# Folding squares on GpSimd, quarter pieces, paired QK bursts and a plan ranked from behind, in a fused attention and highway-FFN kernel

## The chip, the cores and the metric

The kernel runs on one core of a Trainium2 chip. Times are device microseconds (us) of one launch. A profiled execution also gives the span from the first to the last instruction and the duration of each instruction on the engines: TensorE (PE, with its weight loads as PEld), VectorE (DVE), ScalarE (ACT), GpSimd (POOL) and SyncE (SP, which here only issues DMAs).

## The reference

```
q_n = q / (norm(q, axis=-1) + 1e-06);  k_n likewise      # q, k, v: 8 x 12 x 448 x 64
scores = q_n @ k_n^T / tau                               # tau = 0.1
attn = softmax(scores);  y = attn @ v
x = y.transpose(0, 2, 1, 3).reshape(3584, 768)
H = max(x @ w_h, 0);  T = sigmoid(x @ w_t + b_t)
out = T * H + (1 - T) * x
```

Eight batches of twelve heads go through cosine attention, and the 3,584 rows of 768 that come out go through a highway layer with two 768 x 768 weight matrices.

## The kernel before, in words

The attention works in **quads**: four heads of one batch, so 24 quads, three to a batch. For each quad, q and k (t = 0 and t = 1) are loaded in 14 groups of 64 numbers per partition each (`raw`). Their squares (`sq`, 14 x 64 per partition) are made by ACT for q and by POOL for k (DVE in quad 0), and DVE sums each square tile over 64 numbers in two instructions of 7 groups (L338). A reciprocal square root by an integer start value and Newton steps (`rs`, `ta`, L359 to L397) follows, for one quad at a time in the first two batches and for a whole batch later. POOL then multiplies q and k by it in one instruction of 896 numbers per partition each (`qn`, L420). The normalized tiles are turned by PE and copied out of PSUM (quads 0 to 3, `tp`, L440 to L449) or turned by a DMA (L458).

A quad's scores come in seven **chunks**. A chunk is four small matmuls into one of two score buffers in PSUM (`sp`, L505) and one exponential by ACT (`e`, L516). When all seven are there, 84 and then 28 matmuls multiply with v (`u`, L536, one PSUM buffer), and DVE divides by the sums (`rd`, `x`, `xtail`). v is cast to fp16 by DVE (`vm`, L474).

The FFN works in 28 **tiles** of 128 rows: three for each batch, and a fourth after every second batch for the rows left over. A tile is a transpose by PE (`xp`, 6 matmuls), a copy by DVE (`xT`, L642), four quarters of 6 or 7 matmuls of 384 columns (`pt`, L662; 26 per tile), a tanh by ACT (`tt`) or a maximum by DVE (`hm`, L687) behind each quarter, and two closing instructions by DVE per half (`th`, L703, and `o`, L711). The weights come in twelve loads (`wst`), each cast by DVE (`w`, L284), and every FFN matmul waits for all of them (`w_done`). A "batch" below, as a unit of work, is three quads and 3.5 tiles.

The order on each engine is not written by hand. Every operation is handed to a planner (`Plan`) with an engine, a planned duration, a due time (`pri`), and the operations it waits for. `run` simulates the engines greedily, taking at each step the operation that can start first and, among those that can start within 60 ns, the one due first. Its result is the fixed order on each engine. Due times are written out at each operation, mostly as an offset from `slot_t`, the planned start of a quad. The planner also lets POOL and those DVE instructions marked "lock" exclude each other.

Of the kernel before, what the change touches and what calls it, by code (L numbers as in the profile page):

```python
# [20 lines left out]
class Plan:  # L21

    LAT = {"PE": 260, "ACT": 170, "DVE": 150, "POOL": 150, "SP": 0}
    SWITCH = 93

# [22 lines left out]
    def run(self):  # L50
# [17 lines left out]
        ready = {e: [] for e in self.LAT}  # L68

# [18 lines left out]
        while len(order) < len(self.ops):  # L88
            best = None
            for e, L in ready.items():  # L90
# [4 lines left out]
                for r, o in L:  # L95
# [9 lines left out]
                    k = (max(s, t + 60), o.pri, o.n)  # L105
# [34 lines left out]
def kernel(  # L140
# [35 lines left out]
    rd_p = pool("rd", 3)  # L176
    qn_p = pool("qn", N_QN)
# [18 lines left out]
    NV = 2  # L196
    vm_b = [const.tile([128, 6, C, 66], FP16, name=f"vm{i}") for i in range(NV)]
# [37 lines left out]
    def load_qk(Q):  # L235
        b, qd = divmod(Q, NQ)
        ring, wait = P.buf("raw", N_RAW)
        pri = slot_t[Q] - 45
        st["ring_raw", Q] = ring
        got = []  # L240
        for t in range(2):
# [10 lines left out]
            o = op("SP", 60 if Q == 0 and t else 550, pri + 0.01 * t, wait, f, size=1300)  # L252
# [5 lines left out]
    def load_v(b):  # L258
# [10 lines left out]
        o = op("SP", 600, slot_t[NQ * b] - (34 if b else 14), wait, f, size=4000)  # L269
# [3 lines left out]
    w_done = []  # L273

    def load_w(i):
        ring, wait = P.buf("w", N_W)

        def f():
            st["wst", i] = wst_p.tile([128, DM], FP32, name="wst")
            src = (moe_w_h, moe_w_t)[i % 2]  # L280
            nc.sync.dma_start(st["wst", i][:, :], src[(i // 2) * 128 : (i // 2 + 1) * 128, :])

        def g():
            nc.vector.tensor_copy(w_f[i % 2][:, i // 2, :], st["wst", i][:, :])  # L284
# [4 lines left out]
        w_done.append(c)  # L289

    def load_b():
# [6 lines left out]
        a = op("SP", 430, 30, [], f, size=50)  # L298
        w_done.append(op("DVE", 470, 31, [a, o_fb], g))
# [505 lines left out]
```

## Time and profile before

| | us |
|---|---|
| median of 2 runs (346.66 to 347.35) | 347.0 |
| profiled execution: its own time | 349.8 |
| its span | 347.3 |
| PE busy / share of the span | 274.7 / 79% |
| DVE busy / share | 276.4 / 80% |
| ACT busy / share | 196.5 / 57% |
| POOL busy / share | 149.6 / 43% |

The shares are averages over stages that differ: FFN matmuls run only from 82.5 us on, POOL has nothing left to do from about 280 us on, and the last attention work ends near 318 us. The profiled execution is 2.8 us longer than the median of the runs, and 2.5 us of it lie outside the span.

### The profile page before, as it was taken

The numbers are of one execution on the slowest core, as the hardware profiler recorded it, in microseconds if no ns is written. First come the engines' busy times: TensorE is split into PE (matmuls) and PEld (weight loads), VectorE is DVE, ScalarE is ACT, GpSimd is POOL, SyncE is SP. The second block draws the span as 40 slices with busy tenths as digits, with TensorE's granted clock in tenths as the row PEclk, the third lists the DMA queues.
The fourth block names the chain that finished last, engine by engine and source line by source line (L and its number), as shares of the span: only waits on it lengthen the run. The fifth ranks groups of instructions, "written<-read, shape, count | busy, mean of one in ns | idle before, by whom it ended". The sixth has DMA issues, their size and how long they took to land.

```text
span 347.3 us, 10053 instructions
## 1 busy us (share of the span) xinstructions
PE 274.7 (79%) x4312; PEld 153.0 (44%) x4312; DVE 276.4 (80%) x505; ACT 196.5 (57%) x253; POOL 149.6 (43%) x147
## 2 busy tenths in 40 slices
PE   0076785569994889888976999799988999997982
PEld 0044452433551445443542555355454555454541
DVE  4999988956999899999998789776767665665663
ACT  3265865467382568656664586457765676770210
POOL 1438499289693803983386584333232000000000
PEclk9999756555996999999995999899989999998999
DMA  7999195999952767486798954154440641111112
GB/s 285 402 402 359 33 350 148 280 236 301 262 191 63 218 168 254 125 251 120 218 231 205 355 119 100 62 86 100 100 100 6 124 120 47 48 49 47 45 45 91
DMA packets 62318, 58.57 MB, mean 169 GB/s; under 512 B 38722, under 2 KB 57154, under 8 KB 62275
## 3 DMA queue, kind: packets, MB, share of 16 engines
q1 hardware_dynamic: 62002, 57.49, 57.6%
q8 instruction: 33, 0.54, 0.6%
q10 hardware_dynamic: 272, 0.46, 0.4%
q14 instruction: 11, 0.08, 0.1%
HBM read 37.75 MB, written 11.01 MB: 140 GB/s over the span
## 4 chain that ended last, share of the span: by engine, by line
PE 46%; DVE 46%; ACT 3%; issue 2%; DMA 1%; DVEq 0%
PE pt L662 28%; DVE n L338 9%; PE u L536 9%; DVE th L703 8%; PE sp L505 7%; DVE o L711 6%; DVE x L587 4%; DVE hm L687 4%; DVE vm L474 3%; ACT e L516 3%; DVE xT L642 2%; DVE rs L365 2%; PE xp L638 2%; DVE w L284 2%; DMA raw<-in_q_dram 1%
## 5 line engine op out<-in xcount | busy, mean ns | idle before, releaser
L516 ACT ACTIVATE e<-sp 128x896 f16<-128x896 f32 x168 | 149.0, 918 | 88.3 <-PE sp L505 87.9
L662 PE MATMUL pt<-w,xT 128*128 128x384 f16 x672 | 141.7, 342 | 16.8 <-DVE xT L642 14.4
L420 POOL TENSOR_TENSOR qn<-raw,rs 128x896 f16<-128x896 f32 x46 | 83.3, 1831 | 51.1 <-DMA qT<-qn 28.7
L662 PEld LDWEIGHTS <-xT 128*128 128x128 f16 x672 | 59.3, 101 | 70.6 <-issue 23.7
L505 PE MATMUL sp<-qT,qT 64*64 64x448 f16 x672 | 69.0, 426 | 15.7 <-ACT e L516 9.0
L536 PE MATMUL u<-vm,e 64*128 64x65 f16 x2688 | 60.6, 201 | 16.2 <-DVE x L587 14.0
L536 PEld LDWEIGHTS <-e 64*128 64x128 f16 x2688 | 52.3, 101 | 32.9 <-DVE x L587 15.2
L338 DVE TENSOR_REDUCE n<-sq 128x7 f32<-128x448 f16 x96 | 55.2, 605 | 9.4 <-ACT sq L326 7.6
L328 POOL TENSOR_TENSOR sq<-raw 128x896 f16<-128x896 f32 x23 | 40.4, 1761 | 43.4 <-DVE n L338 23.4
L703 DVE SCALAR_TENSOR_TENSOR th<-tt,hm 128x384 f16<-128x384 f16 x56 | 49.5, 890 | 2.7
L682 ACT ACTIVATE tt<-pt 128x384 f16<-128x384 f32 x56 | 27.5, 491 | 41.6 <-PE pt L662 41.5
L687 DVE SCALAR_TENSOR_TENSOR hm<-pt,x 128x384 f16<-128x384 f32 x48 | 26.6, 553 | 26.9 <-PE pt L662 26.4
L505 PEld LDWEIGHTS <-qT 64*64 64x64 f16 x672 | 19.7, 110 | 58.0 <-issue 47.6
L711 DVE SCALAR_TENSOR_TENSOR o<-x,th 128x384 f32<-128x384 f16 x48 | 36.0, 753 | 0.8
L326 ACT ACTIVATE sq<-raw 128x896 f16<-128x896 f32 x24 | 22.7, 951 | 5.8 <-DMA raw<-in_q_dram 5.8
L587 DVE TENSOR_TENSOR x<-u,rd 128x384 f16<-128x384 f32 x48 | 24.4, 549 | 0.5
L474 DVE CAST vm<-vr 128x896 f16<-128x896 f32 x24 | 22.6, 978 | 0.1
L440 PE MATMUL tp<-ident,qn 128*128 128x128 f16 x56 | 7.0, 297 | 17.8 <-DVE qn L420 17.7
L642 DVE COPY xT<-xp 128x768 f16<-128x768 f16 x28 | 15.4, 551 | 6.9 <-PE xp L638 6.6
L569 DVE RECIPROCAL rd<-u 128x12 f32<-128x12 f32 (+1 forms) x48 | 9.7, 202 | 13.4 <-PE u L536 13.1
L662 PE MATMUL pt<-bth,ones_row 128*128 128x384 f16 x56 | 19.1, 340 | 0.0
L391 POOL TENSOR_TENSOR ta<-rs,n 128x84 f32<-128x84 f32 (+1 forms) x18 | 8.0, 445 | 15.9 <-DVE rs L365 15.5
(35 smaller groups left out, 116.6 us busy)
## 6 DMA issues: line engine op xcount, KB each, us to landing
raw<-in_q_dram SPq DMA_DIRECT2D x24, 448.0 KB, 6.1
vr<-in_v_dram SPq DMA_DIRECT2D x8, 1344.0 KB, 7.4
raw<-in_k_dram SPq DMA_DIRECT2D x23, 448.0 KB, 6.0
out_dram<-o SPq DMA_DIRECT2D x24, 384.0 KB, 2.4
wst<-in_moe_w_h_dram SPq DMA_DIRECT2D x6, 384.0 KB, 4.5
wst<-in_moe_w_t_dram SPq DMA_DIRECT2D x6, 384.0 KB, 4.3
out_dram<-o SPq DMA_DIRECT2D x8, 192.0 KB, 2.7
qT<-qn SPq DMA_TRANSPOSE x40, 3.8
```

The source lines that it names most:

```text
L328: (nc.vector if eng == "DVE" else nc.gpsimd).tensor_mul(o, i, i)
L338: nc.vector.reduce_sum(n2[:, qd, g0 : g0 + C], st["sq", Q, t][:, C * part : C * part + C, :], axis=AX.X,)
L420: (nc.vector if eng == "DVE" else nc.gpsimd).tensor_mul(st["qn", Q, t][:, :, :].rearrange("p c (h d) -> p h c d", h=2), st["raw", Q][:, g, ...
L474: nc.vector.tensor_copy(vm[:, 2 * i : 2 * i + 2, :, 0:D], st["vr", b][:, 2 * i : 2 * i + 2, :].rearrange("p i (c d) -> p i c d", c=C),)
L505: nc.tensor.matmul(sp[64 * half : 64 * half + 64, h, 0:S].rearrange("x (c p) -> x c p", c=C), lhsT=kT[hp, ci, 64 * half : 64 * half + 64], ...
L516: nc.scalar.activation(e[:, o : o + 2 * S].rearrange("x (a p c) -> x a p c", a=2, c=C), st["sp", Q, ci][:, :, 0:S].rearrange("x a (c p) -> ...
L536: nc.tensor.matmul(u[:, s, slot * (D + 1) : (slot + 1) * (D + 1)], lhsT=e[sp, o : o + 128], rhs=vm[sp, 2 * qd + h, c, 0 : D + 1], start=(c ...
L587: nc.vector.tensor_mul(st["x", b][:, :, 4 * qd : 4 * qd + 4, :].rearrange("p t (h s) d -> p t h s d", s=2)[:, :, :, s, :], u[:, s, :, 0:D] ...
L662: nc.tensor.matmul(loc["pt", qi][:, :], lhsT=loc["xT"][:, cc, :] if cc < CC else ones_row[:, :], rhs=w_f[w_i][:, cc, ms] if cc < CC else b ...
L687: nc.vector.scalar_tensor_tensor(out=loc["hm"][:, ms], in0=loc["pt", qi][:, :], scalar=0.0, in1=xf()[:, ms], op0=ALU.max, op1=ALU.subtract,)
L703: nc.vector.scalar_tensor_tensor(out=loc["th", mh][:, :], in0=loc["tt"][:, ms], scalar=1.0, in1=loc["hm"][:, ms], op0=ALU.add, op1=ALU.mult,)
L711: nc.vector.scalar_tensor_tensor(out=loc["o"][:, ms], in0=xf()[:, ms], scalar=2.0, in1=loc["th", mh][:, :], op0=ALU.mult, op1=ALU.add,)
```

## The change

1. For quads 6 to 23 both squares are made by ACT. POOL then adds the upper 32 of each 64 squares to the lower 32 (two instructions of 7 groups, `sq` to `fold`, in fp32) and the upper 16 of these to the lower 16 (one instruction over 14 groups). DVE sums what is left, 14 groups of 16, in one instruction. Quads 0 to 5 keep the old sums.
2. POOL's other long instructions are cut: the squares that it still makes (quads 1 to 5) into two of 448, the normalizing products into four of 256 or 192.
3. The score matmuls of two consecutive chunks are issued together, when both score buffers are free.
4. The due time of most operations is no longer written down. It is worked out from behind: what an operation's consumers are due at, less 1.3 times its planned duration and hand-over. The planned spacing of quads is 7.5 us throughout. Loads and casts of the weights have fixed due times, those of `w_t` come first, and a quarter waits only for its own matrix.
5. A tile's transpose is created in the middle of the tile before it, and in quads 0 to 3 both turned tiles are copied by DVE (before, ACT copied one of the two).

```diff
@@ Plan
+    SLACK = 1.3
+    NEAR = {"PE": 100, "ACT": 100, "DVE": 60, "POOL": 60, "SP": 60}
...
+        while back:
+            o = back.pop()
+            due = 1e9 if o.pri is None else o.pri[0] if isinstance(o.pri, tuple) else o.pri
+            for c in outs[o.n] if not isinstance(o.pri, tuple) else ():
+                lat = o.dur + self.LAT[o.eng] + (o.size + 2000 if o.eng == "SP" else 0)
+                due = min(due, c.pri - (self.SLACK * lat / 1000 if o in c.deps else 0))
+            o.pri = due
...
-                    k = (max(s, t + 60), o.pri, o.n)
+                    k = (max(s, t + self.NEAR[e]), o.pri, o.n)
@@ kernel
+    FOLD = 6
+    PAIR = 0
...
-    slot_t = [T0 + (7.6 * Q if Q < NQ else 7.6 * NQ + 9.0 * (Q - NQ)) for Q in range(NQUAD + 2)]
+    slot_t = [14 + 7.5 * Q for Q in range(NQUAD + 2)]
@@ load_w
-            src = (moe_w_h, moe_w_t)[i % 2]
+            src = (moe_w_t, moe_w_h)[i // CC]
...
-        a = op("SP", 430, 13 + 1.4 * i, wait, f, size=1300)
-        c = op("DVE", 470, 14 + 1.4 * i, [a], g, kind="lock")
+        a = op("SP", 430, (12 + 1.8 * i,), wait, f, size=1300)
+        c = op("DVE", 470, (16 + 1.8 * i,), [a], g, kind="lock")
@@ squares
-            eng = "ACT" if t == 0 else ("DVE" if Q == 0 else "POOL")
+            eng = "ACT" if t == 0 or Q >= FOLD else "POOL" if Q else "DVE"
...
+                    nc.gpsimd.tensor_mul(o[:, 0:C, :], i[:, 0:C, :], i[:, 0:C, :])
+            def f2(t=t):
+                o, i = st["sq", Q, t][:, C:NT, :], st["raw", Q][:, NT * t + C : NT * t + NT, :]
+                nc.gpsimd.tensor_mul(o, i, i)
...
+            if Q < FOLD:
+                last = [(C * i, C, D, st_sq(Q, t), [both[i]]) for i in range(2)]
+            else:
+                last = [(0, NT, D // 4, st_fold(Q, t), folds(Q, t, a, ring))]
@@ folds (new)
+                nc.gpsimd.tensor_add(
+                    st["fold", Q, t][:, g, :], sq[:, g, 0 : D // 2], sq[:, g, D // 2 : D]
+                )
+            first.append(op("POOL", 460, None, [a] + ([("first", first)] if first else waitf), f))
+        def h():
+            x = st["fold", Q, t]
+            nc.gpsimd.tensor_add(
+                x[:, :, 0 : D // 4], x[:, :, 0 : D // 4], x[:, :, D // 4 : D // 2]
+            )
+        last = op("POOL", 460, None, first, h)
@@ norms
+            parts = [(0, 2, 0, C)] if eng == "DVE" else [
+                (h, h + 1, c0, c1) for h in range(2) for c0, c1 in ((0, 4), (4, C))
+            ]
...
-                    if t == 0:
-                        nc.scalar.copy(st["qT", Q, t][:, :, :], st["tp", Q, t][:, :, :])
-                    else:
-                        nc.vector.tensor_copy(st["qT", Q, t][:, :, :], st["tp", Q, t][:, :, :])
+                    nc.vector.tensor_copy(st["qT", Q, t][:, :, :], st["tp", Q, t][:, :, :])
@@ quad
+            pair.append((f, needs, ring_s, ring_qT))
+            if Q < PAIR or len(pair) == 2 or g_i == C * NQUAD - 1:
+                fs = [x[0] for x in pair]
...
+                a = op("PE", 400 if len(fs) == 2 else 205, None, sum((x[1] for x in pair), []), both,
+                       kind="quad")
@@ ffn
-                       [c] + ([("first", mms[:1])] if mms else waitq) + w_done, mm, kind="full")
+                       [c] + ([("first", mms[:1])] if mms else waitq) + w_done[w_i], mm, kind="full")
...
+            if qi == 2:
+                later()
```

What the planner makes of this is seen in the order of the instructions. The first place is DVE around the copy of the first FFN tile's transposed rows. Before:

```order
L579 TENSOR_TENSOR xtail<-u,rd 64x2x2x64
L642 COPY xT<-xp 128x768
L284 CAST w_109<-wst 128x768
L284 CAST w_110<-wst 128x768
L474 CAST vm_114<-vr 128x14x64 x3
L338 TENSOR_REDUCE n_672<-sq_968 128x7 x2
L569 RECIPROCAL rd<-u 128x12
```

and with the change:

```order
L669 TENSOR_TENSOR xtail<-u,rd 64x2x2x64
L730 COPY xT<-xp 128x768
L367 TENSOR_REDUCE n_1011<-fold_804 128x14
L367 TENSOR_REDUCE n_1011<-fold_981 128x14
L541 CAST vm_117<-vr 128x14x64 x2
L302 CAST w_112<-wst 128x768
L541 CAST vm_117<-vr 128x14x64
L782 SCALAR_TENSOR_TENSOR hm<-pt,x 128x384
L798 SCALAR_TENSOR_TENSOR th<-tt,hm 128x384
```

Both stand behind the third quad. Before, 4 of 12 weight casts stand ahead of the copy and the first `hm` comes 30 rows after it (two more quads lie between, on PE 18 chunks and 224 matmuls with v). Now 11 of 12 stand ahead of it, the first `hm` comes six rows after it, and one chunk pair lies on PE between the transpose and the end of the tile's first quarter.

The second place is POOL ahead of quad 6, the first of the third batch (`sq` squares, `ta` and `rs` the Newton steps for a batch, `qn` normalizing). Before:

```order
L328 TENSOR_TENSOR sq_1156<-raw 128x896
L393 TENSOR_TENSOR ta<-ta,rs 128x84
L395 TENSOR_SCALAR ta<-ta 128x84
L397 TENSOR_TENSOR rs<-ta,rs 128x84
L420 TENSOR_TENSOR qn_1186<-raw,rs 128x2x7x64
L420 TENSOR_TENSOR qn_1282<-raw,rs 128x2x7x64
L420 TENSOR_TENSOR qn_1291<-raw,rs 128x2x7x64
```

and with the change:

```order
L454 TENSOR_TENSOR ta<-ta,rs 128x84
L394 TENSOR_TENSOR fold_1398<-sq_1348 128x224
L456 TENSOR_SCALAR ta<-ta 128x84
L394 TENSOR_TENSOR fold_1398<-sq_1348 128x224
L458 TENSOR_TENSOR rs<-ta,rs 128x84
L394 TENSOR_TENSOR fold_1472<-sq_1364 128x224
L486 TENSOR_TENSOR qn_1503<-raw,rs 128x4x64 x2
L486 TENSOR_TENSOR qn_1511<-raw,rs 128x4x64 x2
L486 TENSOR_TENSOR qn_1503<-raw,rs 128x3x64 x2
L486 TENSOR_TENSOR qn_1511<-raw,rs 128x3x64 x2
```

The same stretch is now short instructions, and the squares are gone from it.

The third place is ACT near the middle of the program (`sq` squares, `e` exponentials, `tt` tanh). Before:

```order
L682 ACTIVATE tt<-pt 128x384
L326 ACTIVATE sq_3316<-raw 128x896
L516 ACTIVATE e_117<-sp 128x896 x2
L682 ACTIVATE tt<-pt 128x384
L516 ACTIVATE e_117<-sp 128x896 x3
L682 ACTIVATE tt<-pt 128x384
L516 ACTIVATE e_117<-sp 128x896
```

and with the change:

```order
L777 ACTIVATE tt<-pt 128x384
L343 ACTIVATE sq_3358<-raw 128x896
L586 ACTIVATE e_119<-sp 128x896 x2
L777 ACTIVATE tt<-pt 128x384
L343 ACTIVATE sq_3416<-raw 128x896
L586 ACTIVATE e_119<-sp 128x896
L586 ACTIVATE e_120<-sp 128x896
L343 ACTIVATE sq_3487<-raw 128x896
L586 ACTIVATE e_120<-sp 128x896 x2
```

Exponentials now come in twos, mostly with a square or a tanh between the twos.

## Rows read from the trace of the kernel before

**Rows 1.** The page's busy time: us, share of span, instructions.

```profile
PE 274.7 (79%) x4312; PEld 153.0 (44%) x4312; DVE 276.4 (80%) x505; ACT 196.5 (57%) x253; POOL 149.6 (43%) x147
```

**Rows 2.** Stages: start:end, length, busy PE, PEld, DVE, ACT, POOL, clock, DMA, GB/s.

```profile
57.00:82.50 25.50, 16.86 (x297) 9.03 (x294) 21.02 (x36) 16.63 (x21) 17.79 (x19) 0.50 0.90 259
82.50:220.00 137.50, 116.87 (x1826) 63.16 (x1823) 125.80 (x215) 83.44 (x110) 82.53 (x73) 0.92 0.72 192
220.00:341.50 121.50, 113.00 (x1708) 62.89 (x1704) 79.62 (x154) 65.16 (x88) 15.71 (x14) 0.96 0.28 70
```

**Rows 3.** DVE and PE around the first FFN tile: start, us, instruction.

```profile
56.96 0.56 DVE L642 COPY xT<-xp 128x768 f16<-128x768 f16 x1
...
82.47 2.10 PE L662 MATMUL pt<-w,xT 128*128 128x384 f16 x6
```

**Rows 4.** PE in the late stage, start, us, instruction: one batch.

```profile
270.94 0.38 PE L505 MATMUL sp<-qT,qT 64*64 64x448 f16 x4
271.26 1.51 PE L536 MATMUL u<-vm,e 64*128 64x65 f16 x84
...
290.59 0.57 PE L505 MATMUL sp<-qT,qT 64*64 64x448 f16 x8
291.10 0.62 PE L536 MATMUL u<-vm,e 64*128 64x65 f16 x28
...
304.02 1.51 PE L536 MATMUL u<-vm,e 64*128 64x65 f16 x84
```

**Rows 5.** Groups by line: busy us, mean ns, idle before (releaser).

```profile
L338 DVE TENSOR_REDUCE n<-sq 128x7 f32<-128x448 f16 x96 | 55.2, 605 | 9.4 <-ACT sq L326 7.6 <-POOL sq L328 1.6
L703 DVE SCALAR_TENSOR_TENSOR th<-tt,hm 128x384 f16<-128x384 f16 x56 | 49.5, 890 | 2.7
L711 DVE SCALAR_TENSOR_TENSOR o<-x,th 128x384 f32<-128x384 f16 x48 | 36.0, 753 | 0.8
L474 DVE CAST vm<-vr 128x896 f16<-128x896 f32 x24 | 22.6, 978 | 0.1
L326 ACT ACTIVATE sq<-raw 128x896 f16<-128x896 f32 x24 | 22.7, 951 | 5.8 <-DMA raw<-in_q_dram 5.8
L391 POOL TENSOR_TENSOR ta<-rs,n 128x84 f32<-128x84 f32 (+1 forms) x18 | 8.0, 445 | 15.9 <-DVE rs L365 15.5
```

**Rows 6.** DVE, start, us: five sums in a row; then `th` beside POOL.

```profile
101.97 4.00 DVE L703 SCALAR_TENSOR_TENSOR th<-tt,hm 128x384 f16<-128x384 f16 x2
...
109.70 2.72 DVE L338 TENSOR_REDUCE n<-sq 128x7 f32<-128x448 f16 x5
```

**Rows 7.** POOL, start, us: products of 896 and small Newton steps.

```profile
7.81 1.68 POOL L328 TENSOR_TENSOR sq<-raw 128x896 f16<-128x896 f32 x1 [6.51 <-DMA raw<-in_k_dram]
...
43.62 0.45 POOL L393 TENSOR_TENSOR ta<-ta,rs 128x28 f32<-128x28 f32 x2
...
50.53 3.33 POOL L420 TENSOR_TENSOR qn<-raw,rs 128x896 f16<-128x896 f32 x2
...
99.95 7.57 POOL L420 TENSOR_TENSOR qn<-raw,rs 128x896 f16<-128x896 f32 x4
```

**Rows 8.** One line's instructions: ns min/median/max, first and last start.

```profile
L703 DVE SCALAR_TENSOR_TENSOR th<-tt,hm x56: 520/559/2044, 87.7 to 341.9; 128x384 f16<-128x384 f16 x56
L711 DVE SCALAR_TENSOR_TENSOR o<-x,th x48: 487/558/2036, 88.8 to 337.3; 128x384 f32<-128x384 f16 x48
L474 DVE CAST vm<-vr x24: 610/621/2111, 25.0 to 256.5; 128x896 f16<-128x896 f32 x24
```

**Rows 9.** Waits in the whole span: engine, line, releaser, us, times, longest.

```profile
ACT e L516 <- PE sp L505: 87.9, 70, 6.1
PE u L536 <- DVE x L587: 14.0, 12, 2.1
```

**Rows 10.** ACT and the end, start, us: exponentials in a row; the last matmul's reader.

```profile
21.02 3.35 ACT L516 ACTIVATE e<-sp 128x896 f16<-128x896 f32 x4 [1.42 <-PE sp L505]
...
341.25 0.56 DVE L687 SCALAR_TENSOR_TENSOR hm<-pt,xtail 128x384 f16<-128x384 f32 x1 [0.30 <-PE pt L662]
```

More of the change, by code (lines that the diff above doesn't have):

```diff
@@ L251, in f @@
                 )
-            o = op("SP", 60 if Q == 0 and t else 550, pri + 0.01 * t, wait, f, size=1300)
+            o = op("SP", 60 if Q == 0 and t else 550, None, wait, f, size=1300)
             wait = [("first", [o])] + wait if not got else wait
@@ L347, in squares, with st_sq, st_fold, folds @@
         return reds
-    def rsqrt(b, qd, n, reds, due):
+    def st_sq(Q, t):
+        return lambda: st["sq", Q, t]
+    def st_fold(Q, t):
+        return lambda: st["fold", Q, t]
+    def folds(Q, t, a, ring):
+        ringf, waitf = P.buf(f"fold{t}", 2)
+        first = []
+        for i in range(2):
+            def f(i=i):
+                if i == 0:
+                    st["fold", Q, t] = fold_p.tile([128, NT, D // 2], FP32, name=f"fold{t}")
+                g = slice(C * i, C * i + C)
+                sq = st["sq", Q, t]
+                nc.gpsimd.tensor_add(
[8 more added lines that the diff above has]
+        last = op("POOL", 460, None, first, h)
+        ring += first
+        ringf += first + [last]
+        st["ring_fold", Q, t] = ringf
+        return [last]
+    def rsqrt(b, qd, n, reds):
+        due = None
         eng = "DVE" if b == 0 else "POOL"
@@ L482, in cast_v @@
         st["vm", b] = (ring, outs)
+    pair, late = [], []
     def quad(Q):
@@ L493, in quad @@
         exps = {}
-        for ci in range(7):
+        for ci in range(C):
+            g_i = C * Q + ci
             ring_s, wait_s = P.buf("sp", 2)
@@ L520, in g, with both @@
                 )
-            a = op("PE", 205, t_step(Q, ci) - 3, wait_s + [st["turned", Q, t] for t in range(2)], f,
-                   kind="quad")
-            x = op("ACT", 810, t_step(Q, ci), wait_e + [a], g)
-            ring_s += [a, x]
-            for r in ring_qT:
-                r.append(a)
+            needs = wait_s + [st["turned", Q, t] for t in range(2)]
+            pair.append((f, needs, ring_s, ring_qT))
+            if Q < PAIR or len(pair) == 2 or g_i == C * NQUAD - 1:
+                fs = [x[0] for x in pair]
+                def both(fs=fs):
+                    for x in fs:
+                        x()
+                a = op("PE", 400 if len(fs) == 2 else 205, None, sum((x[1] for x in pair), []), both,
+                       kind="quad")
+                for x in pair:
+                    x[2].insert(0, a)
+                    for r in x[3]:
+                        r.append(a)
+                for y in late:
+                    y.deps.append(a)
+                pair.clear()
+                late.clear()
+                mine = [a]
+            else:
+                mine = []
+            x = op("ACT", 810, t_step(Q, ci), wait_e + mine, g)
+            if not mine:
+                late.append(x)
+            ring_s.append(x)
             ring_e.append(x)
@@ L690, in fa @@
                     )
[L691 removed]
+                e = op("DVE", 470, None, [mms[-1]] + waitf, fa)
             ringq.append(e)
```

133 lines of the change are left out of this document (78 added, 55 removed).

## The prediction

> **What bounds the kernel now.** I read the busy times first, then the same by stages, then the order of work on PE and DVE at two places, then the prices of the instructions that the change touches. On the average, PE and DVE are level, 274.7 and 276.4 of 347.3 us [rows 1], and the average hides three different kernels [rows 2]. From 57 to 82.5 us no FFN matmul runs: PE is busy 16.9 of 25.5 us at a granted clock of 0.50, the lower of the two levels (1.2 of 2.4 GHz). From 82.5 to 220 us DVE is busy 125.8 of 137.5 us (91%) and PE 116.9 (85%): there DVE sets the pace. From 220 us on DVE drops to 79.6 of 121.5 us and PE is at 113.0 (93%): there PE sets it. So two things cost time: the FFN starts late, and DVE holds PE back until its sums and GpSimd's long instructions are done with.
>
> The first shows at one place. The first tile's rows are copied at 56.96 us and its first matmul runs at 82.47 us [rows 3]. In the order, 8 of the 12 weight casts stand behind that copy, and the matmul waits for all twelve.
>
> The second has two parts. DVE's sums over 64 take 55.2 us [rows 5]. And the closing instructions of the FFN and the casts of v have medians of 0.56, 0.56 and 0.62 us but maxima of 2.04, 2.04 and 2.11 [rows 8]. The stretch at 102 us shows why: two `th` take 4.00 us while POOL does four products of 896 in 7.57 us [rows 6, 7]. Each of these DVE instructions stands until the running POOL instruction has ended. Means less medians give what this costs: 56 x 0.33 + 48 x 0.20 + 24 x 0.36 = 36.5 us [rows 5, 8].
>
> **The change, engine by engine.** *DVE.* A sum over 448 numbers takes 0.54 us when five stand in a row (2.72 / 5) [rows 6]. Of 96, 72 go: -39.2 us. In their place 36 sums over 224 numbers come. No row shows one: it is not dearer than 0.54 and, if it goes by the count of numbers, 0.27. I take 0.30, nearer the second, since the rows that differ in count on POOL also shrink with it: +10.8 us (9.8 to 19.6). Four more copies of turned tiles, priced like the copy of 0.56 [rows 3]: +2.2. The waiting for POOL is for a piece of some 0.55 us instead of 1.67, a third, but POOL is busy in a larger share of the time (205 of some 310 us instead of 150 of 347, 1.5 times): 36.5 x 0.33 x 1.5 = 18 us are left, 18 go (none to 24). Together DVE falls from 276 to about 231 us.
>
> *POOL.* Two products of 896 take 3.33 us, so 1.665 each; two steps on 28 numbers take 0.45, so 0.225 each [rows 7]. The line through both is 0.18 us and 1.66 ns a number: 0.55 for 224 numbers, 0.60 for 256, 0.50 for 192, 0.92 for 448. The 46 normalizing products go from 1.665 to 2.20 us each: +24.6. Adds: 18 quads x 2 x 3 x 0.55 = +59.4. Eighteen squares go: -30.0, and five are cut in two: +0.9. POOL rises from 149.6 to about 204 us. All of it lies beside other work as long as the normalized tiles are there before PE asks; POOL's cover is that squares of a batch are all made two quads (third batch) to four quads (later ones) ahead of its first scores in the new order. If that cover goes, see the last rival.
>
> By the Trainium skill (GPSIMD Engine Reference, § 4.1 Engine selection) elementwise adds belong on VectorE, since GpSimd is about twice as slow, and a reduction along the free dimension belongs there too; by that rule the folding is on the wrong engine. The trace agrees that it is a bad exchange in busy time, 59 us of adds for 28 us of sums. It is paid from POOL's idle 198 us [rows 1], so by the rows the rule does not decide here; by the rule it would make the last rival.
>
> *ACT.* Eighteen more squares at 0.95 us [rows 5], less four copies of about the same length: +13 us, 210 in all. The cost that is not busy time is the wait in each pair: exponentials in a row start 0.84 us apart (3.35 / 4) [rows 10] and need no gap as long as the other score buffer is full. Now both must be empty before the next pair starts: 0.51 us of matmuls and two hand-overs stand between the twos. In a batch of 10.5 pairs that is 10.5 x (1.68 + 0.51 + some 0.25 of hand-overs) = 25.6 us, and the 6 squares and 7 tanh of a batch (9 us) partly fall in those gaps, so 28 to 31 us.
>
> *PE.* One chunk's matmuls take 0.32 us until the next group starts (270.94 to 271.26), two together 0.51 (290.59 to 291.10) [rows 4]. A pair saves 0.13, 84 pairs 10.9 us. A batch at PE's pace takes 32.8 us (271.26 to 304.02) [rows 4], so now 32.8 - 10.5 x 0.13 = 31.4. ACT's ring of 28 to 31 and DVE's and POOL's sums (231 and 204 over eight batches, the first one and a half heavier) lie just under it.
>
> **The sum.** (a) The first tile's copy stays at about 57 us: DVE has 7 more weight casts and 4 more copies ahead of it, 6 sums fewer, and shorter waits. The first FFN matmul follows at 58 us instead of 82.5, since only the first matrix is waited for. (b) From there 8 batches at 31.4 less the attention of the three quads that are done, each 1.51 + 0.62 + 3.5 x 0.51 = 3.9 us [rows 4]: 251 - 11.7 = 239.5 us. (c) Behind the last matmul the kernel of before needs 6.1 us (341.2 to 347.3) [rows 10]: 6. (d) Until the squares are done, about two thirds of (b), all five resources lie close together and the orders are fixed. Before, PE was busy 85% there against 93% [rows 2], 9% longer. With the DVE load down I keep half: 160 x 0.047 = 7.5 us. The span is then 58 + 239.5 + 6 + 7.5 = 311 us. With the 2.5 us outside the span that is 313.5 us against the profiled execution's 349.8, and since that execution lies 2.8 us above the median of the runs, **311 us** against the median of 347.0.
>
> **The rivals.**
>
> *PE's pace throughout.* No loss in (d) and a front part 5 us shorter, because the waits for POOL shrink there too: 311 - 12 = 299 us. For it: in the late stage ACT and DVE are far from full. Against: there POOL has 15.7 us of work in 121.5 [rows 2]; in the new order it works nearly throughout. Chance 0.15.
>
> *The old pace stays, or the FFN does not start early.* If ACT's ring or PE's waits for DVE's `x` (14.0 us before, one buffer for `u`) [rows 9] keep the full 9%, and the first tile comes 8 us late, it is 311 + 7.5 + 8 = 327. If the change does not do what it says at all in front, because GpSimd's many pieces delay the first batches, FFN matmuls start at 82.5 us with five quads done: 82.5 + 251 - 19 + 6 + 7.5 = 328 us of span, 328 against the median too. For it: exponentials already wait 87.9 us for score matmuls [rows 9], and now each pair must. Chance 0.22.
>
> *GpSimd becomes the bound.* Its pieces may not get shorter with their size. There are 302 of them (184 products, 108 adds, 10 half squares), at most 4 x 8.0 = 32 us of Newton steps beside them [rows 5] (four groups of 18, this one the costliest), and POOL's first square starts at 7.8 us [rows 7]. In the order five tiles stand on PE behind the last score pair; with the last quad's exponentials before them and the 6 us of (c) the last products must be done some 40 us before the end (an estimate), at 271 us in the forecast. That leaves 231 us for 302 pieces, 0.77 each. A piece that also gives DVE a turn, as the four products did (7.57 / 4 less 1.665, 0.23) [rows 7], takes 0.78, and at most half of them can, since DVE has some 150 such instructions. From 0.77 on each further 0.1 us costs 30 us: at 0.89 the gain is gone, and from 0.92 on, 356 us, the kernel is slower than before. Against it: a step on 28 numbers takes 0.225 [rows 7], so most of the time does go with the count. Chance 0.06 for slower, 0.07 for a time within the band of no change.
>
> **Chances and range.** About 2% (7 us) is what a measurement of this kernel can tell from no change. The forecast (303 to 320) has 0.50, PE's pace 0.15, the old pace 0.22, GpSimd 0.13. Faster by over 2% (below 340) is 0.87 by these, and I give 0.85 with 0.09 within 2% and 0.06 slower, since in a fixed order one late engine is enough. The range from 295 to 333 takes in the two cases beside the forecast, the dearer sums (9 us of DVE, mostly covered) and no gain in the waiting (18 us of DVE, half of it covered), and leaves out the last rival.
>
> **What would show it.** Right: the first `pt` matmul near 58 us; `th` with a maximum near 1.1 us instead of 2.04; 36 sums from `fold` at some 0.3 us; POOL's pieces at 0.5 to 0.6 us and 205 us of busy time; DVE near 231 us; score matmuls in eights; a batch every 31 to 34 us from 60 us on; the clock off its lower level from then on. Wrong: PE waiting for turned tiles, or `qn` pieces above 0.8 us (GpSimd); long waits of ACT for score matmuls with PE idle at the same time (the pairs); weight casts or the first copy late (the front).

## The result and the profile after

The changed kernel takes 313.17 us (median of 2 runs, 313.09 to 313.26) against 347.0: a ratio of 0.9025, 95% interval 0.8985 to 0.9065. Its profiled execution took 313.1 us, of which the span is 310.8. The times of experiments 7 and 8 below are medians without one slow run each (321.52 and 315.99 us). First its busy time and the head of its chain of waits, from the page, to be held against [rows 1].

```profile
PE 253.0 (81%) x4312; PEld 145.0 (47%) x4312; DVE 230.0 (74%) x473; ACT 203.1 (65%) x267; POOL 226.0 (73%) x380
...
POOL 43%; PE 27%; DVE 17%; DMA 5%; issue 4%; SPq 1%; ACT 1%; DVEq 0%; POOLq 0%; ACTq 0%
```

DVE came out as forecast (231), POOL did not (204). GpSimd now has the largest share of the chain that ended last; in the kernel before that share was PE 46% and DVE 46%. The share is not steady: in a second profile of the same kernel (experiment 5) POOL has 22%. The stages (columns as in [rows 2]):

```profile
0.00:54.00 54.00, 28.95 (x504) 17.30 (x505) 43.91 (x106) 32.94 (x38) 38.56 (x71) 0.87 0.95 329
54.00:80.00 26.00, 20.53 (x365) 11.69 (x363) 19.95 (x40) 19.60 (x26) 25.62 (x45) 1.00 0.94 258
80.00:120.00 40.00, 29.72 (x509) 16.79 (x502) 24.38 (x46) 23.62 (x31) 36.83 (x66) 0.83 0.80 173
120.00:180.00 60.00, 56.00 (x1028) 31.57 (x1026) 48.80 (x98) 49.92 (x67) 58.96 (x94) 1.00 0.85 225
180.00:240.00 60.00, 55.37 (x963) 30.45 (x957) 47.15 (x93) 44.28 (x60) 58.07 (x96) 0.97 0.59 139
240.00:300.00 60.00, 57.73 (x941) 34.52 (x938) 40.74 (x85) 31.68 (x45) 7.97 (x13) 1.00 0.33 77
```

The fifth busy column is the new thing: from 54 to 240 us POOL is busy 179.5 of 186 us (96%). The stage that clocked at 0.50 and held no FFN matmul [rows 2] now runs at 1.00. The weak stage is 80 to 120 us, where PE does 29.7 of 40. PE around the first FFN tile, to be held against [rows 3]:

```profile
53.81 0.66 PE L757 MATMUL pt<-w,xT 128*128 128x384 f16 x3 [0.75 <-DVE xT L730]
...
58.33 0.32 PE L757 MATMUL pt<-w,xT 128*128 128x384 f16 x1 [1.79 <-DVE w L302]
```

The groups of the change by line (busy us, mean ns, idle before), and the lines that close the FFN, to be held against [rows 5, 7]:

```profile
L486 POOL TENSOR_TENSOR qn<-raw,rs 128x256 f16<-128x256 f32 (+1 forms) x184 | 111.5, 642 | 5.7 <-DMA qT<-qn 3.5 <-DVE rs L450 1.9 <-issue 0.2
L394 POOL TENSOR_TENSOR fold<-sq 128x224 f32<-128x224 f16 x72 | 49.5, 705 | 0.9 <-ACT sq L343 0.9
L400 POOL TENSOR_TENSOR fold<-fold 128x224 f32<-128x224 f32 x36 | 26.2, 749 | 0.0
...
L367 DVE TENSOR_REDUCE n<-fold 128x14 f32<-128x224 f32 x36 | 13.4, 380 | 9.8 <-POOL fold L400 9.5
L798 DVE SCALAR_TENSOR_TENSOR th<-tt,hm 128x384 f16<-128x384 f16 x56 | 37.7, 674 | 3.4
L806 DVE SCALAR_TENSOR_TENSOR o<-x,th 128x384 f32<-128x384 f16 x48 | 33.0, 688 | 1.1
L541 DVE CAST vm<-vr 128x896 f16<-128x896 f32 x24 | 19.4, 832 | 0.0
```

and the same lines one instruction at a time (ns min/median/max, first and last start), to be held against [rows 8]:

```profile
L798 DVE SCALAR_TENSOR_TENSOR th<-tt,hm x56: 546/581/1044, 59.4 to 305.4; 128x384 f16<-128x384 f16 x56
L394 POOL TENSOR_TENSOR fold<-sq x72: 599/609/990, 46.2 to 220.7; 128x224 f32<-128x224 f16 x72
L400 POOL TENSOR_TENSOR fold<-fold x36: 654/663/2196, 54.1 to 223.1; 128x224 f32<-128x224 f32 x36
L486 POOL TENSOR_TENSOR qn<-raw,rs x184: 500/613/1199, 17.5 to 248.2; 128x256 f16<-128x256 f32 x92, 128x192 f16<-128x192 f32 x92
L586 ACT ACTIVATE e<-sp x168: 902/917/1015, 17.3 to 277.8; 128x896 f16<-128x896 f32 x168
```

`th`, `o` and `vm` together took 108.1 us [rows 5] and take 90.1. Most DVE instructions now stand for about one short POOL piece at most, but one does not. At 94 us, on DVE, on POOL and on PE (start, us, instruction, idle before):

```profile
94.17 3.76 DVE L420 TENSOR_SCALAR rs<-n 128x84 int32<-128x84 int32 x1
...
98.09 0.55 DVE L782 SCALAR_TENSOR_TENSOR hm<-pt,x 128x384 f16<-128x384 f32 x1
```

```profile
93.67 4.20 POOL L486 TENSOR_TENSOR qn<-raw,rs 128x256 f16<-128x256 f32 x8
```

```profile
98.69 2.08 PE L757 MATMUL pt<-w,xT 128*128 128x384 f16 x6 [3.34 <-DVE hm L782]
```

A step that is 0.2 us long elsewhere ran for 3.76 us, until POOL's row of eight pieces had ended; `hm` stood behind it, and PE waited 3.34 us for `hm`. This belongs to the weak stage.

### The profile page after: what moved, and what is told of

It is laid out like the page before. It is cut to its first block, busy times and chain, and to the rows that moved or that the text cites. A ratio compares the mean times of both kernels' runs of the same rounds, so it can differ in the third digit from the quotient of the medians.

```text
span 310.8 us, 10324 instructions
## 1 busy us (share of the span) xinstructions
PE 253.0 (81%) x4312; PEld 145.0 (47%) x4312; DVE 230.0 (74%) x473; ACT 203.1 (65%) x267; POOL 226.0 (73%) x380
## 4 chain that ended last, share of the span: by engine, by line
POOL 43%; PE 27%; DVE 17%; DMA 5%; issue 4%; SPq 1%; ACT 1%; DVEq 0%; POOLq 0%; ACTq 0%
POOL qn L486 20%; PE pt L757 18%; POOL fold L394 10%; POOL fold L400 6%; PE u L626 4%; DVE n L367 4%; PE sp L575 3%; DMA raw<-in_q_dram 3%; POOL ta L452 2%; DVE vm L541 2%; POOL ta L454 2%; DVE rs L420 2%; POOL rs L458 2%; DVE th L798 2%; DMA raw<-in_k_dram 2%
## 5 line engine op out<-in xcount | busy, mean ns | idle before, releaser
L586 ACT ACTIVATE e<-sp 128x896 f16<-128x896 f32 x168 | 145.2, 920 | 59.2 <-PE sp L575 59.0
L757 PE MATMUL pt<-w,xT 128*128 128x384 f16 x672 | 133.7, 332 | 12.7 <-DVE hm L782 9.7
L486 POOL TENSOR_TENSOR qn<-raw,rs 128x256 f16<-128x256 f32 (+1 forms) x184 | 111.5, 642 | 5.7 <-DMA qT<-qn 3.5
L575 PE MATMUL sp<-qT,qT 64*64 64x448 f16 x672 | 54.8, 394 | 10.7 <-ACT e L586 4.0
L394 POOL TENSOR_TENSOR fold<-sq 128x224 f32<-128x224 f16 x72 | 49.5, 705 | 0.9 <-ACT sq L343 0.9
L343 ACT ACTIVATE sq<-raw 128x896 f16<-128x896 f32 x42 | 39.9, 965 | 10.3 <-DMA raw<-in_q_dram 10.3
L798 DVE SCALAR_TENSOR_TENSOR th<-tt,hm 128x384 f16<-128x384 f16 x56 | 37.7, 674 | 3.4
L575 PEld LDWEIGHTS <-qT 64*64 64x64 f16 x672 | 14.2, 108 | 34.0 <-issue 23.5
L400 POOL TENSOR_TENSOR fold<-fold 128x224 f32<-128x224 f32 x36 | 26.2, 749 | 0.0
L367 DVE TENSOR_REDUCE n<-fold 128x14 f32<-128x224 f32 x36 | 13.4, 380 | 9.8 <-POOL fold L400 9.5
L510 PE MATMUL tp<-ident,qn 128*128 128x128 f16 x56 | 7.1, 299 | 14.3 <-DVE qn L486 13.9
```

What stands on the lines that cost most here:

```text
L394: nc.gpsimd.tensor_add(st["fold", Q, t][:, g, :], sq[:, g, 0 : D // 2], sq[:, g, D // 2 : D])
L400: nc.gpsimd.tensor_add(x[:, :, 0 : D // 4], x[:, :, 0 : D // 4], x[:, :, D // 4 : D // 2])
L486: (nc.vector if eng == "DVE" else nc.gpsimd).tensor_mul(st["qn", Q, t][:, :, :].rearrange("p c (h d) -> p h c d", h=2)[:, h0:h1, c0:c1, :] ...
L575: nc.tensor.matmul(sp[64 * half : 64 * half + 64, h, 0:S].rearrange("x (c p) -> x c p", c=C), lhsT=kT[hp, ci, 64 * half : 64 * half + 64], ...
L586: nc.scalar.activation(e[:, o : o + 2 * S].rearrange("x (a p c) -> x a p c", a=2, c=C), st["sp", Q, ci][:, :, 0:S].rearrange("x a (c p) -> ...
L757: nc.tensor.matmul(loc["pt", qi][:, :], lhsT=loc["xT"][:, cc, :] if cc < CC else ones_row[:, :], rhs=w_f[w_i][:, cc, ms] if cc < CC else b ...
```

## The experiments

Twelve kernels ran in three groups of four (1 to 4, 5 to 8, 9 to 12), each group on one chip with its own runs of the kernel before (medians 343.06, 348.14 and 344.24 us). The same kernel came out at 0.8922 in one group and 0.9135 in another, so differences of 1 to 2% are read only between kernels of one group. In the second group the runs of the kernel before spread from 343.43 to 350.04 us, as far apart as many kernels here, so kernels of that group are compared by their times. Unless said otherwise, each edit is made to the changed kernel.

**1. No folding.**

```diff
-    FOLD = 6
+    FOLD = 24
```

> The changed kernel without the folding (quads 6 to 23 make the squares of k on GpSimd in halves again, VectorE sums over 64). By rows of the changed kernel 108 adds go (49.5 + 26.2 us of GpSimd) and 18 squares of 2.1 us come (+38), so GpSimd falls from 226 to about 188 us; VectorE gains 72 sums of 0.54 and loses 36 of 0.37, +26 us to 256; ScalarE loses 17 us. Theory 1 (the folding pays because VectorE held TensorE back): slower than the changed kernel's 313 us, about 322. Theory 2 (in the changed kernel GpSimd, busy 19 to 20 of every 20 us from 40 to 240 us, sets the pace): faster, 295 to 305, until TensorE's own pace binds.

Measured: 307.84 us, ratio 0.8977 (0.8911 to 0.9042). DVE rose to 250.0 us, POOL fell to 191.0, and POOL's last product started at 233.3 us instead of 248.2. That is far from theory 1 (322) and a little above theory 2 (295 to 305). Taking the folding out costs nothing that this shows. No DVE instruction of this kernel lasts longer than 1.28 us.

**2. No pairs.**

```diff
-    PAIR = 0
+    PAIR = 24
```

> The changed kernel with the score matmuls issued chunk by chunk again (84 more groups on TensorE, 0.13 us each, 11 us). Theory 1 (TensorE's pace after the first tile): slower by most of these 11 us, 320 to 325. Theory 2 (GpSimd sets the pace until 240 us): TensorE's extra work is hidden until then and shows only in the last 60 us, so 313 to 317. If the wait of ScalarE in each pair was a cost of its own, it would be faster than 313.

Measured: 329.79 us, 0.9597 (0.9511 to 0.9682). That is above every range that was expected, and looks like 20 us for the pairs. The trace says otherwise for most of it. DVE, POOL and PE (start, us, instruction, idle before):

```profile
61.52 7.08 DVE L541 CAST vm<-vr 128x896 f16<-128x896 f32 x1
...
102.91 8.85 DVE L798 SCALAR_TENSOR_TENSOR th<-tt,hm 128x384 f16<-128x384 f16 x1
```

```profile
61.66 0.60 POOL L394 TENSOR_TENSOR fold<-sq 128x224 f32<-128x224 f16 x1
62.23 4.19 POOL L486 TENSOR_TENSOR qn<-raw,rs 128x256 f16<-128x256 f32 x8
...
103.02 2.31 POOL L394 TENSOR_TENSOR fold<-sq 128x224 f32<-128x224 f16 x4
105.29 1.90 POOL L400 TENSOR_TENSOR fold<-fold 128x224 f32<-128x224 f32 x3
107.14 4.20 POOL L486 TENSOR_TENSOR qn<-raw,rs 128x256 f16<-128x256 f32 x8
```

```profile
71.39 0.95 PE L626 MATMUL u<-vm,e 64*128 64x65 f16 x28 [5.74 <-DVE x L677]
...
113.40 2.08 PE L757 MATMUL pt<-w,xT 128*128 128x384 f16 x6 [8.20 <-DVE hm L782]
```

Two DVE instructions were held through long rows of POOL pieces, the second through fifteen, and PE waited 13.9 us behind them (5.74 + 8.20). The new order happened to put them there; this run prices the holds more than the pairs, and where the remaining 6 us come from stays open.

**3. Whole products** (pieces undone, folding and pairs kept).

```diff
-            parts = [(0, 2, 0, C)] if eng == "DVE" else [
-                (h, h + 1, c0, c1) for h in range(2) for c0, c1 in ((0, 4), (4, C))
-            ]
+            parts = [(0, 2, 0, C)]
...
-                    nc.gpsimd.tensor_mul(o[:, 0:C, :], i[:, 0:C, :], i[:, 0:C, :])
+                    nc.gpsimd.tensor_mul(o, i, i)
```

> The changed kernel with the normalizing products in one instruction of 896 and the squares of quads 1 to 5 in one, the folding kept. GpSimd saves 46 x (2.57 - 1.83) = 34 us, and each VectorE instruction that needs the shared port waits for up to 1.8 us again instead of 0.6. Theory 1: VectorE's waits rise by some 15 to 18 us and it is slower, 318 to 325. Theory 2: GpSimd's 34 us less count for more, 300 to 308.

Measured: 318.32 us, 0.9272 (0.9194 to 0.9351). POOL's work fell to 198.6 us and the time rose all the same; DVE rose to 248.0. DVE's three groups in this kernel:

```profile
L806 DVE SCALAR_TENSOR_TENSOR o<-x,th 128x384 f32<-128x384 f16 x48 | 42.4, 886 | 0.8
L798 DVE SCALAR_TENSOR_TENSOR th<-tt,hm 128x384 f16<-128x384 f16 x56 | 41.4, 741 | 2.6
L541 DVE CAST vm<-vr 128x896 f16<-128x896 f32 x24 | 23.7, 999 | 0.0
```

Together 107.5 us, the sum of the kernel before (108.1). With pieces it is 90.1: the 18 us are the pieces'. In time theory 1 holds (318 to 325), but beside folding the pieces are worth only some 5 us against the changed kernel of the other groups (313.2 and 313.7).

**4. The new order alone** (edits 1 to 3 together).

> The new planning alone: no folding, no pairs, whole GpSimd instructions, so the instructions of the kernel before in the new order (with its earlier weights and its later transposes). Theory 1: the first FFN matmul comes at about 54 us instead of 82.5, worth some 17 us net, but VectorE has its 276 us of work back, so about 328. Theory 2: GpSimd is at about 150 us and out of the way, so the gain of the changed kernel is mostly this, 312 to 320. If the planning were worth nothing it would be 345 to 347.

Measured: 326.97 us, 0.9538 (0.9462 to 0.9615), so 16 us, as theory 1 had it (about 328). The first FFN matmul ran at 57.2 us, 25 us earlier than before.

**5. The changed kernel again**, as the companion of the next three.

> The changed kernel itself, for times on the same chip as the three kernels beside it: 313 us, a ratio to the kernel before of 0.90 to 0.915.

Measured: 313.68 us, 0.8997 (0.8912 to 0.9082), with the same hold of 3.75 us at 94.8 us. POOL was as busy (226.5 us), but the chain of this profile, 3 us longer, is another:

```profile
PE 47%; POOL 22%; DVE 21%; issue 4%; DMA 3%; ACT 2%; SPq 0%; DVEq 0%; POOLq 0%
```

**6. One fold step** (two adds of 224 for each tile; DVE sums 32 numbers a group).

```diff
-        last = op("POOL", 460, None, first, h)
...
-        return [last]
+        return first
...
-                last = [(0, NT, D // 4, st_fold(Q, t), folds(Q, t, a, ring))]
+                last = [(0, NT, D // 2, st_fold(Q, t), folds(Q, t, a, ring))]
```

> The changed kernel with one of the two steps of folding: GpSimd adds 64 squares to 32, VectorE sums 32 numbers (14 groups, 448 numbers) instead of 16. GpSimd loses 36 adds of 0.75 us (226 to about 200 us), VectorE gains 36 x some 0.23 us (230 to 238). Theory A (TensorE sets the pace once VectorE waits little, and GpSimd only has to be in time): within 3 us of the changed kernel. Theory B (GpSimd, busy nearly all of 40 to 240 us, sets the pace): 26 us less of it, 303 to 308 us.

Measured: 309.88 us (308.27 to 310.84), 0.8897 (0.8824 to 0.8970). Its slowest run is below the fastest of experiment 5 (312.24). POOL 198.3 us, DVE 234.8, last product at 234.5 us. The second fold step costs POOL 28 us, saves DVE 5, and the kernel is 1.2% faster without it. The time lies between the two theories: more than theory A's 3 us, less than theory B's 303 to 308. A long hold does not explain the difference, for this kernel has one too. On POOL, DVE and PE:

```profile
86.21 4.19 POOL L480 TENSOR_TENSOR qn<-raw,rs 128x256 f16<-128x256 f32 x8
86.94 3.52 DVE L414 TENSOR_SCALAR rs<-n 128x84 int32<-128x84 int32 x1
92.08 0.40 PE L720 MATMUL xp<-ident,x 128*128 128x128 f16 x2 [6.49 <-DVE x L671]
```

**7. Late weights.** Weight loads wait for the loads of quads 4 to 9, and every quarter for all twelve casts.

```diff
+        a = op("SP", 430, (12 + 1.8 * i,), wait + st["got", 4 + i // 2 if i < 10 else 9], f, size=1300)
...
+                       [c] + ([("first", mms[:1])] if mms else waitq) + w_done[0] + w_done[1], mm, kind="full")
...
-        if Q == 1:
+        if Q == 9:
             for i in range(2 * CC):
                 load_w(i)
```

> The changed kernel with the weight loads tied behind the loads of q and k of quads 4 to 9, and every FFN quarter waiting for all twelve casts again, so that the first FFN matmul follows the fourth quad and not the third. Theory A: the first matmul comes 12 to 16 us later, in which TensorE does one more quad's attention (4 us) and a few chunk pairs, so 321 to 326 us. Theory B (GpSimd's pace until 240 us): the later FFN is caught up while GpSimd holds the attention back, 313 to 316.

Measured: 315.51 us, 0.9066 (0.8957 to 0.9175), as theory B had it. The first FFN matmul ran at 67.7 us instead of 54.5. FFN work alone (tile `pt`: start:end, length, busy PE, DVE, ACT; clock, DMA, GB/s), first late weights, then experiment 5:

```profile
54.00:80.00 26.00, 8.65 (x33) 1.11 (x2) 1.15 (x3) 0.67 0.74 193
80.00:120.00 40.00, 20.11 (x110) 4.44 (x8) 4.37 (x9) 1.00 0.84 193
```

```profile
54.00:80.00 26.00, 13.99 (x65) 2.76 (x5) 2.46 (x5) 0.89 0.89 251
80.00:120.00 40.00, 15.45 (x68) 2.57 (x5) 2.47 (x5) 0.79 0.74 170
```

By 120 us the later start has been made up: 143 FFN matmuls against 133. Its order also has no long hold, which in the changed kernel costs some 3 us, so that 13 us of start are worth some 2 us here (hardly more than the runs differ, 315.06 to 316.12 against 312.24 to 315.56), or 5 with an estimated 3 us for the hold.

**8. Order and pieces, without folding and pairs** (edits 1 and 2).

> No folding and no pairs; the quarter pieces and the new planning stay. Beside the run without folding (308 us) it shows what pairs are worth where VectorE isn't caught by the run of GpSimd pieces that cost the run without pairs 14 us (two VectorE instructions of 7.1 and 8.9 us). Theory A: the 11 us of TensorE that pairs save, so 317 to 320. If pairs were worth the whole difference of 17 us, 324 to 326; if they were worth nothing but for those two waits, 307 to 311.

Measured: 310.48 us, 0.8922 (0.8835 to 0.9008): what the changed kernel has, or a little less, without two of its parts. That is where pairs were expected to be worth nothing (307 to 311), not 11 us (317 to 320). Longest DVE hold 1.98 us.

**9. Pieces alone**, put into the kernel before with its written due times.

```diff
@@ norms of the kernel before
-            a = op(eng, 1000 if eng == "DVE" else 1800, due + t, wait + [rs_op] + st["got", Q], f,
+            parts = [(0, 2, 0, C)] if eng == "DVE" else [
+                (h, h + 1, c0, c1) for h in range(2) for c0, c1 in ((0, 4), (4, C))
+            ]
...
+                    eng, 1000 if eng == "DVE" else 40 + 1.95 * n, due + t,
```

> The kernel before with its written due times, sums, pairs and weights as they were; only GpSimd's normalizing products are cut into four and its squares into two. Theory 1, plan and pieces add up: the ratio of planning alone to planning with pieces was 0.9538 to 0.8922, so pieces alone should give 0.935 to 0.95, with closing instructions (th) at most 1.1 us instead of 2.04. Theory 2, the old due times leave DVE no slack and the FFN still starts at 82 us, so that shorter holds are only taken up by other waits: 0.97 to 1.00.

Measured: 326.96 us, 0.9522 (0.9488 to 0.9557). One stage (columns as in the table of stages) and `th` one by one:

```profile
54.00:80.00 26.00, 10.71 (x257) 6.95 (x254) 21.40 (x35) 9.64 (x12) 21.75 (x38) 0.54 0.94 247
```

```profile
L722 DVE SCALAR_TENSOR_TENSOR th<-tt,hm x56: 540/559/1283, 84.6 to 318.4; 128x384 f16<-128x384 f16 x56
```

The front is as bad as before (clock 0.54, first `th` at 84.6 us), and still 16 us are gained behind it. `th`, `o` and `vm` take 87.0 us here. Order alone 0.9538, pieces alone 0.9522: the product is 0.908, and both together gave 0.8922 and (next) 0.9135. They add up, as theory 1 said, though 0.9522 lies just outside its 0.935 to 0.95 and `th` reached 1.28 us where 1.1 was expected.

**10. Order and pieces again, with six runs.**

> Planning and pieces without folding and without pairs, once more with more rounds. Theory 1, both left-out parts are worth nothing: 0.885 to 0.897, at or below the changed kernel's 0.9025. Theory 2, the first look was the luck of one chip: 0.90 to 0.91.

Measured: 314.13 us (311.97 to 314.84), 0.9135 (0.9093 to 0.9176). The second theory was nearer. By the medians it equals the changed kernel of the other groups (313.2 and 313.7), by the ratios it is 1% slower, and the group before had it 1% faster: the two parts left out are worth at most 1% together.

**11. One fold step, no pairs** (edits 2 and 6).

> One fold step (DVE sums 32 numbers per group instead of 16 or 64), score matmuls chunk by chunk. Theory 1, neither pairs nor folding matter as long as no DVE instruction is held through a row of pieces: 0.885 to 0.897, longest DVE hold about 2 us. Theory 2, with folding GpSimd is so full that, without pairs, rows of eight and sixteen pieces form behind each other again as in the changed kernel without pairs: holds of 7 to 9 us and 0.92 to 0.96.

Measured: 309.96 us, 0.9028 (0.8982 to 0.9073), 1.3% below experiment 10. It lies between the two theories, nearer the first. One fold step is worth that much against none; pairs are not needed for it. POOL is busy 199.7 us, DVE 230.4, and the longest hold is 2.93 us.

**12. GpSimd's measured durations in the planner.**

```diff
-                    eng, 1000 if eng == "DVE" else 40 + 1.95 * n, None,
+                    eng, 1000 if eng == "DVE" else 240 + 1.66 * n, None,
...
-            a = op(eng, {"ACT": 840, "DVE": 1000, "POOL": 860}[eng], None,
+            a = op(eng, {"ACT": 840, "DVE": 1000, "POOL": 930}[eng], None,
```

(and edits 1 and 2; the second half square's 860 also became 930)

> As planning and pieces without folding and pairs, and the planner is given GpSimd's pieces at the durations measured beside the other engines (0.665 and 0.56 us instead of 0.54 and 0.41; half squares 0.93 instead of 0.86). Theory 1, GpSimd has slack enough at 193 us of work, so the order hardly cares: within 1% of the kernel without folding and pairs. Theory 2, a planner that believes GpSimd faster than it is places consumers too early, and each arrives to a wait: 2 to 3% faster, below 0.875.

Measured: 321.90 us, 0.9370 (0.9323 to 0.9417), 2.5% slower than experiment 10, against both theories. POOL's waits in it, and then in experiment 10 (engine, line, releaser: us in total, times, longest):

```profile
POOL sq L347 <- DVE n L367: 21.8, 6, 9.2
POOL sq L347 <- DMA raw<-in_k_dram: 17.4, 2, 10.9
```

```profile
POOL sq L347 <- DVE n L367: 10.2, 4, 3.9
POOL sq L347 <- DMA raw<-in_k_dram: 9.6, 4, 6.4
```

POOL had less to do (184.5 against 190.4 us) and was done 19 us later, its last product at 258.6 us instead of 239.4, because in this order it stood longer at the head of its queue. One `th` was also held for 4.17 us (98.82 us), and PE waited 4.40 us behind it. Better durations did not make a better order; why the planner put those squares there stays open.

## Why the prediction was right, and where it was not

The time, 311 forecast and 313.2 measured, is inside its own 303 to 320. The account behind it holds in part. The gain is that of two parts: the new order alone gives 16 us (experiment 4), the pieces alone 16 (experiment 9), and both together reach the changed kernel's time without folding and pairs (experiments 8 and 10). The forecast counted on all four. That folding paid by relieving DVE, and pairs by relieving PE, is what did not show.

**(a) The early start came; in the changed kernel it was worth at most about half its price.** The first FFN matmul ran at 53.8 us; 58 was forecast. The sum puts all of it on the path: 24.5 us, less the attention of two quads that is then still to be done (2 x 3.9), so some 17 us net. Experiment 7 takes 13 us of the start away with one quad more done ahead of it, so that the sum would lose 9; it loses 2 to 5. The step that failed is adding the start to the length of the batches, as if the FFN had to run at an even pace behind it. FFN matmuls fill what attention leaves free on PE, and a late start leaves more of them for gaps that stand open anyway. How much the start alone is worth where GpSimd is less busy was not tried: without folding, the whole new order, start included, is worth 13 us beside pieces (experiments 9 and 10, 326.96 and 314.13 us). The end followed the end of attention. From the last exponential's start to the end of the span it is 33.0 us here (310.8 - 277.8) and 35.7 before (347.3 - 311.6); in experiments 1, 2, 8, 9 and 12 it is 32.5 to 36.1. The order fixes this: 125 FFN matmuls start behind that point in every kernel with the new order, 115 in the kernel before and in experiment 9. Nearly the whole change lies ahead of that point.

**(b) The pace of a batch held only late, and the pairs' share in it did not show.** In the changed kernel (PE: start, us, instruction), and in the late stage of experiment 10, which has no pairs:

```profile
58.59 1.51 PE L626 MATMUL u<-vm,e 64*128 64x65 f16 x84
...
105.04 0.84 PE L626 MATMUL u<-vm,e 64*128 64x65 f16 x42
...
239.98 1.51 PE L626 MATMUL u<-vm,e 64*128 64x65 f16 x84
...
259.00 0.57 PE L575 MATMUL sp<-qT,qT 64*64 64x448 f16 x8
...
271.30 1.51 PE L626 MATMUL u<-vm,e 64*128 64x65 f16 x84
```

```profile
241.45 1.51 PE L626 MATMUL u<-vm,e 64*128 64x65 f16 x84
...
273.01 1.50 PE L626 MATMUL u<-vm,e 64*128 64x65 f16 x84
```

Three quads lie between the late rows: 31.3 us, 31.4 forecast. But without pairs it is 31.6 there, with six transposes less (0.5 us) and four score matmuls more (0.4 us) on PE, so some 0.4 of the 1.4 us that the forecast gave to pairs shows (an estimate). And between the two early rows, three quads too, it is 46.5 us, with PE busy for 33.0; from 105 us on any three quads in a row took 28 to 36. The sign named, 31 to 34 us from 60 us on, did not come. PE's busy time falls with pairs (252.9 us in experiment 1, 259.4 in 10), but no pair of kernels with and without them, and without long holds, differs by more than the groups do. Whether pairs are worth nothing or some 1% of the time stays open.

**(c) and (d).** From the first FFN matmul to the end it took 257.0 us (310.8 - 53.8); (b), (c) and (d) gave 253. Behind the last `hm` it took 6.0 us (304.76 to 310.8), as (c) said. With (b) as forecast, (d), the loss while all resources lie close, was 11.5 us rather than 7.5, and the 80 to 120 us stage alone left PE idle for 10.3. So the start was 4 us early and the loss 4 us larger, and the span came to 310.8 for 311. That closeness is luck, and the more so since a start 13 us later changed the time by only 2 to 5 us. The 2.8 us by which the profiled execution lay above the median did not come back (313.09 against 313.17), which makes the 2 us between forecast and measurement.

**DVE.** 230.0 us for 231 (the terms as written add up to 232). The sums over 224 cost 0.38 each instead of 0.30 (+3 us). The waits, 18 us of gain forecast, came to exactly that on the three lines (108.1 to 90.1). Experiments 3 and 9 give it wholly to the pieces. This step was right, and the sum underrates it: alone it is worth 16 us, and its price on POOL (34 us more busy time in experiment 9, 183.4 against 149.6) cost nothing that shows there. Beside folding, where POOL is nearly full, some 5 us of it are left (experiment 3).

**ACT.** 203.1 us for 210: the exponentials' busy time fell from 149.0 to 145.2, and 59.0 us of waiting for scores are left of 87.9 [rows 9]. ACT's ring was not the bound.

**POOL.** 226.0 us for 204. The products took 0.64 a piece on the average instead of 0.55 (+10 us), the adds 0.71 and 0.75 instead of 0.55 (+16). Alone they take 0.50 to 0.66 (the minima). The rest, some 26 us, lies in 72 of the 292 pieces, all of them beside a DVE instruction, mostly `o`, `th` or `vm`. The line through a product of 896 and a Newton step of 28 [rows 7] fitted the products alone (0.50 for 192, 0.61 for 256) and not the adds that write fp32 (0.60 and 0.65 for 0.55).

**The last rival was nearer than its chance.** It wants the products done 40 us before the end. They were done at 248.7 of 310.8 us: 29.6 us from the last product's start to the last exponential's, and 33.0 from there. With that tail of 62 us the point from which GpSimd decides is not 0.77 us a piece but about 0.69 (an estimate: 310.8 less 62, 7.8 and 32, over 302), within the 0.64 to 0.75 that was measured; busy for 96% of 54 to 240 us, GpSimd was close to it. The lead of the last product over the last exponential by kernel:

| kernel | POOL busy | last product | last exponential | lead | span |
|---|---|---|---|---|---|
| before | 149.6 | 261.1 | 311.6 | 50.5 | 347.3 |
| changed | 226.0 | 248.2 | 277.8 | 29.6 | 310.8 |
| 5, changed again | 226.5 | 251.7 | 280.7 | 29.0 | 313.8 |
| 7, late weights | 224.7 | 249.7 | 280.5 | 30.8 | 313.7 |
| 2, no pairs | 220.0 | 270.2 | 296.2 | 26.0 | 328.7 |
| 12, measured durations | 184.5 | 258.6 | 288.5 | 29.9 | 321.0 |
| 1, no folding | 191.0 | 233.3 | 273.4 | 40.1 | 306.4 |
| 6, one fold step | 198.3 | 234.5 | 274.6 | 40.1 | 307.8 |
| 10, no folding, no pairs | 190.4 | 239.4 | 279.5 | 40.1 | 312.1 |
| 3, whole products | 198.6 | 235.5 | 283.3 | 47.8 | 316.3 |
| 9, pieces alone | 183.4 | 241.7 | 288.0 | 46.3 | 324.1 |

In experiments 4, 8 and 11 the lead is 43.1, 38.9 and 40.6. In experiment 1, at 40.1, POOL has time to wait for its tiles to come free (waits, columns as in experiment 12):

```profile
POOL qn L486 <- DMA qT<-qn: 17.3, 6, 5.6
```

In the changed kernel the same wait is 3.5 us (row of `qn` above), and the lead is 29 to 31 in its three profiles with two fold steps, pairs and pieces (changed, 5 and 7). A short lead alone does not show that GpSimd's work sets the pace: in experiment 12 it is 29.9 although POOL has only 184.5 us of work and no share of the chain, in experiment 2 POOL has 8%, and experiment 3 is slow with a lead of 47.8.

The folding turned 20 us of DVE's work into 35 of POOL's (230.0 against 250.0, 226.0 against 191.0), and nothing gained shows. That POOL's load costs time in the changed kernel is shown by experiments 5 and 6 alone: a single step takes 28 us of work from GpSimd and is 1.2% faster, 3.8 us. Experiment 1 is 2 us faster still (307.84, in another group), which is within what groups differ by; and it has no long hold, where the changed kernel and experiment 6 each have one. No kernel separates the load from the holds, so whether a single step also beats no folding with pairs stays open.

The Trainium skill (GPSIMD Engine Reference, § 4.1 Engine selection) puts elementwise adds on VectorE. The runs agree as far as the second step goes; the first gained 1.3% without pairs (experiments 10 and 11), on a GpSimd that had been busy 61% of the span.

**What would have shown it.** `th` at a maximum of 1.04 us (1.1 named), 36 sums, scores in eights and the clock off its lower level (0.83 to 1.00 by stage from 54 us on) came. POOL's busy time missed (226 for 205), and its pieces, 0.64 on the average, lay above the 0.5 to 0.6 named for the right case and below the 0.8 named for the wrong one.

## What to carry to other kernels

Cut the long instructions of an engine that another has to wait for: it cost GpSimd 34% more time for the same products and still gained 5% by itself, with the due times unchanged (experiment 9). Before work is moved to an idle engine, work out when that engine must be done, counted back from the end through everything that still follows its last result, and not from its share of the span. An early start of work that fills gaps is worth only what that work cannot make up later; measure it by delaying it.

## What the runs showed of the hardware

A DVE instruction that has to wait for GpSimd mostly waits for about one instruction: in the changed kernel `th` takes at most 1.04 us beside pieces, before it took 2.04 beside whole products [rows 8]. But some were held through a row of pieces: through the last seven of a row of eight (3.76 us in the changed kernel), and through fifteen (8.85 us in experiment 2), as long as POOL went from one piece to the next without a gap. The two of experiment 2 had begun 0.14 and 0.11 us before POOL started its next instruction (61.52 and 61.66, 102.91 and 103.02), the one of the changed kernel about 0.07 us. That is not what decides it: the holds of 3.52, 2.93 and 4.17 us in experiments 6, 11 and 12 began 0.32 to 0.41 us before POOL's next piece. The Trainium skill (SBUF — State Buffer, § SBUF: two separate sides) has the side that starts first keep the shared port pair for one whole instruction, and the other block; by that the longest hold beside pieces would be about one piece, and these rows show more. What decides it stays open: no kernel was tried that breaks up the rows of pieces by itself.
